# Late v, half masks, transposes in two PSUM banks, and two more chunks transposed by the crossbar, in a fused retention and Mish feed-forward kernel

## The chip, the core and the metric

One core of one Trainium2 chip. The time is the device time of one execution in microseconds (us). The kernel before takes 314.44 us (median of 3 runs, 314.15 to 315.28). A difference of under 2% counts as "same".

## The reference, cut to what matters

```python
# q, k, v: (8 batches, 8 heads, 576 positions, 64)
scores = q @ k.T / sqrt(64)
ret    = scores * Dmat[None]           # Dmat[h,i,j] = gamma_h ** (i-j) for i >= j, else 0
x      = (ret @ v) -> (4608 tokens, 512)
h = x @ w_in                            # 512 x 2048
g = h * tanh(softplus(h))               # Mish
out = g @ w_out                         # 2048 x 512, float32
```

The 576 positions are cut in chunks of 128 tokens, 36 chunks in all, two chunks of two batches being a pair (pair 7 is chunks 14 and 15). Inside a chunk the scores are computed whole; what earlier positions give comes through a running state (the sum of k times v). The feed-forward part runs over groups of four chunks, and it is nearly all of TensorE's work. A projection is full-width when it takes all 512 tokens of a group at once. In the first groups, where not all tokens are there yet, a chunk's own projections are cut in four quarters, between which other jobs are placed.

Of the kernel before, what the change touches and what calls it, by code (L numbers as in the profile page):

```python
# [11 lines left out]
BF16 = mybir.dt.bfloat16  # L12
# [5 lines left out]
def kernel(  # L18
# [30 lines left out]
    nF = d_ff // P  # L49
    KC = d_model // P  # L50
    NCH = 4
    NPE = 16


    chunks = []
# [69 lines left out]
    def load_w_in(f, nf):  # L125
        cols = ds(P * f, P * nf)
        nc.gpsimd.dma_start(out=w_in_t[:, :, cols], in_=w_in_r[:, :, cols])
# [19 lines left out]
    def await_load(n, x):  # L147

        m, u = divmod(n, 2)
        nc.gpsimd.tensor_copy(seen, pairs[m][x][0:1, u, H - 1, 0:1])  # L150

    def load_v(n):
        (b, i0, _), = chunks[n]
        nc.gpsimd.dma_start(out=pairs[n // 2]["v"][:, n % 2], in_=v[b, :, ds(i0, P), :].rearrange("h p d -> p h d"))
# [28 lines left out]
    mask1 = consts.tile([P, 2, NP, P], F32)  # L183
    for h in range(H):
        nc.scalar.activation(mask1[:, h // NP, h % NP, :], dif, AX.Exp, scale=log_g[h])
    load_v(0)

    pos = consts.tile([P, 5], F32)
    nc.gpsimd.iota(pos, pattern=[[P, 5]], base=0, channel_multiplier=1,
# [20 lines left out]
                            base=0, pattern=[[1, P]], channel_multiplier=-1)  # L210
    nc.gpsimd.tensor_copy(mask2, mask)
    nc.gpsimd.memset(mask2[0:64, 64:P], 0.0)
    load_v(1)

    st_sum = {}
    st_sb = {}
# [49 lines left out]
    def step_t(n):  # L266

        m, u = divmod(n, 2)
        r = pairs[m]
        if "qk" not in r:  # L270
            r["qk"] = tr.tile([P, 2, 2, NP, P], BF16, name="qkT", bufs=3)
        if n >= NPE:
            nc.sync.dma_start_transpose(out=r["qk"].rearrange("p i u n t -> p (i u n) t"),
                                          in_=r["qks"].rearrange("p i u h d -> p (i u h d)"))
            return
        tp = ps_sc.tile([P, 4, NP, P], BF16, name="sc")[:, 0:2]
        for i in range(2):
            flat = r["qks"][:, i, u].rearrange("p h d -> p (h d)")
            for p in range(NP):
                nc.tensor.transpose(tp[:, i, p, :], flat[:, ts(p, P)], ident)  # L280
        for i, copy in enumerate((nc.scalar.copy, nc.vector.tensor_copy)):
            copy(r["qk"][:, i, u], tp[:, i])  # L282

    def step_n(m):

        r = pairs[m]
        kp = ps_sc.tile([P, 4, NP, P], BF16, name="sc")[:, 0:2]
        for u in range(2):
            for p in range(NP):
                nc.tensor.transpose(kp[:, u, p, :], r["qk"][:, 1, u, p, :], ident)  # L290
        r["ks"] = tok.tile([P, 2, H, D], BF16, name="ks", bufs=2)
        for u in range(2):
            nc.vector.tensor_tensor(
                by_slots(r["ks"][:, u]), by_slots(kp[:, u].rearrange("p s (r d) -> p (s r) d", r=2)),
                gk[:, place(2 * m), :].rearrange("p (r s) -> p r s", r=2).unsqueeze(3).to_broadcast([P, 2, NP, D]),
                op=OP.mult)

    def step_s(n):

        m, u = divmod(n, 2)  # L300
        qk = pairs[m]["qk"]
        sc = scores_tile()
        for p in range(NP):
            for e in range(2):
                r = ds(64 * e, 64)
                nc.tensor.matmul(sc[:, e, p, :], lhsT=qk[r, 1, u, p, :], rhs=qk[r, 0, u, p, :],  # L306
                                 start=True, stop=True)
        sm = tr.tile([P, 2, NP, P], BF16, name="sm")
        nc.vector.tensor_tensor(  # L309
            sm.rearrange("p e n i -> p (e n) i"), sc.rearrange("p e n i -> p (e n) i"),  # L310
            mask1.rearrange("p e n i -> p (e n) i") if n < NCH else
            (mask if len(chunks[n]) == 1 else mask2).unsqueeze(1).to_broadcast([P, 2 * NP, P]), op=OP.mult)
        pairs[m][u] = (sc, sm)

    def step_k(m):

        if m >= n_pairs or len(chunks[2 * m]) > 1:
            return
        b, i0, _ = chunks[2 * m][0]
        ks, vs = pairs[m]["ks"], pairs[m]["vs"]  # L320

        if m < 6:
            st = ps_sc.tile([P, 2, 2, NP, 64], F32, name="sc")[:, 0]
        else:
            st = ps_h.tile([P, 2, NP, 64], F32, name="hp")
        for u in range(2):
            for p in range(NP):
                for e in range(2):
                    nc.tensor.matmul(st[ds(64 * e, 64), u, p, :], lhsT=ks[:, u, 2 * p + e, :],  # L329
                                     rhs=vs[:, u, 4 * e + p, :],  # L330
                                     start=(u == 0 and p == 0), stop=True, skip_group_check=True)
        if i0 == 0:
            st_sum[b] = tr.tile([P, 2, NP, 64], F32, name="st")
            nc.vector.tensor_copy(st_sum[b], st)
        else:
            nc.vector.tensor_tensor(st_sum[b], st_sum[b], st, op=OP.add)  # L336
        ssb = tr.tile([P, 2, NP, 64], BF16, name="ssb", bufs=6)
        (nc.vector.tensor_copy if m < 4 else nc.scalar.copy)(ssb, st_sum[b])  # L338
        for u in range(2):
            st_sb[b + u, i0 + P] = ssb[:, u]  # L340

# [37 lines left out]
        xt, s = x_of(n)  # L379
        nc.scalar.copy(xt[:, :, ts(s, P)].rearrange("p (e g) i -> p e g i", e=2), ot)  # L380

    def pair_o(m):

        sc = pairs[m][1][0]
        ot = sc.rearrange("p e (g u) i -> p e g u i", g=2)
        step_k(m)
        for u in range(2):
            within(pairs[m]["vs"][:, u], pairs[m][u][1], ot[:, :, :, u, :], u == 0)
        for u in range(2):
            across(2 * m + u, ot[:, :, :, u, :])  # L390
        xt, s = x_of(2 * m)
        nc.vector.tensor_copy(xt[:, :, ds(s * P, 2 * P)].rearrange("p n (u i) -> p n u i", u=2),  # L392
                              sc.rearrange("p e (g u) i -> p (e g) u i", g=2))


    gts = {}
# [70 lines left out]
    def one(n, steps):  # L467
        for step in steps:
            if step == "P":
                step_p(n // 2, (n % 2,))  # L470
            else:
                {"T": step_t, "S": step_s, "O": step_o}[step](n)

    def first(n, steps):
        for step in steps:
            if step in "qk":
                cast_first(n, "qk".index(step))
            elif step in "QK":
                turn_first(n, "QK".index(step))
            else:  # L480
                {"V": cast_v, "S": step_s, "O": step_o}[step](n)

    first(0, "qQkK")
    await_load(0, "k")
    load_v(2)
    first(1, "q")
    keep_warm(3)
    first(0, "VS")
    first(1, "Qk")
    keep_warm(3)  # L490
    await_load(1, "k")
    load_v(3)
    await_load(2, "q")
    load_w_in(0, 2)
    first(1, "K")
    first(0, "O")
    first(1, "V")
    first(2, "q")
    keep_warm(3)
    first(1, "S")  # L500
    first(2, "Qk")
    keep_warm(3)
    await_load(2, "k")
    load_w_in(2, 2)
    load_w_in(4, 4)
    load_w_in(8, 4)
# [26 lines left out]
    for i in range(4, nF):  # L533
        if i == 6:
            step_n(0)
        elif i == 8:
            step_k(0)
        elif i == 9:
            step_n(1)
        elif i == 10:  # L540
            one(4, "P")
        elif i == 12:
            one(4, "T")
        elif i == 13:
            one(4, "S")
        elif i == 14:
            one(5, "P")
        elif i == 15:
            one(4, "O")
        g1(0, i)  # L550

    load(6)
    for n in range(4, 8):
        for fb in range(4):
            if n < 7:
                if fb == 1:
                    one(n + 1, "T")
                elif fb == 2:
                    one(n + 1, "S")
                    if n % 2 == 0:  # L560
                        step_k(n // 2)
                    if n < 6:
                        one(n + 2, "P")
                elif fb == 3:
                    one(n + 1, "O")
            g1_chunk(n, fb)
    load(7)

    def visit(m, w):

        n = 2 * m
        if w == 0:
            if m > 4:
                step_p(m)
            if 2 * m + 2 < NPE:
                load(m + 4)
        elif w == 2:
            if m == 5:
                step_k(1)
            one(n, "T")  # L580
        elif w == 3:
            one(n + 1, "T")
        elif w == 5:
            one(n, "S")
            one(n + 1, "S")
        elif w == 7 and m < 6:
            pair_o(m)

    def cross(m):

        step_t(2 * m)
        nc.gpsimd.tensor_copy(seen, pairs[m]["qk"][0:1, 0, 0, 0, 0:1])  # L592
# [15 lines left out]
        g2(1, i)  # L608
    for i in range(nF):
        visit(6 + i // 8, i % 8)  # L610
        if i == 6:
            step_p(8)
        elif i == 8:
            cross(8)
            load(11)
        g1(2, i)
        if i % 8 == 7:
            pair_o(6 + i // 8)
            if i == 15:
                scores(8)  # L620
            for j in range(4):
                g2(1, 8 + i // 2 - 3 + j)
# [50 lines left out]
```

## The kernel before: what the change touches

Scores need q and k transposed. For the chunks from 4 up to `NPE` TensorE does it, from there on a crossbar transpose on SyncE's DMA queue:

```python
NPE = 16
def step_t(n):                                   # transposes of chunk n
    if n >= NPE:
        nc.sync.dma_start_transpose(out=r["qk"]..., in_=r["qks"]...)   # whole pair
        return
    tp = ps_sc.tile([P, 4, NP, P], BF16, name="sc")[:, 0:2]            # PSUM, one bank
    ...                                          # 2 x 4 TensorE transposes of 128x128
    for i, copy in enumerate((nc.scalar.copy, nc.vector.tensor_copy)):
        copy(r["qk"][:, i, u], tp[:, i])         # q's half by ScalarE, k's by VectorE
```

The start loads q and k on SyncE and v and the weights on GpSimd's queue, in an order that small waits on GpSimd (`await_load`) hold in place. In the third group of the feed-forward, small jobs are placed between projections (`w` counts them):

```python
def visit(m, w):
    if w == 0:
        if m > 4: step_p(m)                      # scale q and k of pair m (VectorE)
        if 2 * m + 2 < NPE: load(m + 4)          # loads of a later pair
    elif w == 2: one(2*m, "T")
    ...
def cross(m):                                    # crossbar transpose, GpSimd waits for it
    step_t(2 * m)
    nc.gpsimd.tensor_copy(seen, pairs[m]["qk"][...])

for i in range(nF):                              # third group: pairs 6 and 7
    visit(6 + i // 8, i % 8)
    if i == 6:   step_p(8)
    elif i == 8: cross(8); load(11)
    g1(2, i)                                     # first projection of 128 columns, Mish
    if i % 8 == 7:
        pair_o(6 + i // 8)                       # outputs of the pair
        ...
        g2(...)                                  # second projection; stores on SyncE
```

## Time and profile before

| | before |
|---|---|
| time, profiled run | 314.46 us (span 312.8) |
| TensorE busy | 300.0 us, 96% |
| VectorE, ScalarE busy | 123.4 and 136.0 us |
| granted TensorE clock | 1.00 |
| DMA share, 0 to about 95 us | near full |
| first scores / first projection / first full-width projection | 8.52 / 18.07 / 22.61 us |
| scores of chunks 14 / 16 / 18 start | 104.16 / 108.58 / 124.02 us |

A kernel that is 96% TensorE can gain only by closing TensorE's gaps or by taking work from it, and a part of a change that does not reach TensorE shows nothing. In the timelines (start, duration, engine and line, operation) PE is TensorE's matmuls, PEld its weight loads, DVE VectorE, ACT ScalarE, POOL GpSimd and SP SyncE; a q behind the name marks the engine's issuing queue, L273 is a line of the kernel, and brackets at the end give the idle time before an instruction and what ended it. First the chain that ended last, from the page: shares of the span by engine, then by line.

```profile
PE 89%; ACT 4%; DVE 3%; issue 2%; DMA 1%; SPq 1%; ACTq 0%; DVEq 0%
```

DMA is 1% of it. Second, the timeline of SyncE's queue where a pair is transposed: start, duration, engine and line, operation.

```profile
113.45 0.35 SPq L462 DMA_DIRECT2D out_dram<-res  x1
114.65 1.95 SPq L273 DMA_TRANSPOSE qkT<-qks  x1
```

### The profile page before, as it was taken

What the parts mean: (1) busy time and instruction counts of PE and PEld (TensorE: products, weight loads), DVE (VectorE), ACT (ScalarE), POOL (GpSimd) and SP (SyncE); (2) the same over time, 40 slices, a digit from 0 to 9 for tenths busy, and PEclk for the clock granted to TensorE, in tenths of its full rate; (3) what the DMA queues carried; (4) which work ended last, traced back from release to release, by engine and by line L of the source; (5) the groups of instructions that cost most, each with busy time, mean ns of one, the idle gap of its engine ahead of it and who ended that gap; (6) DMA issues with size and microseconds to landing.
All of it is one profiled execution on the core that took longest, in us unless ns stands there. A gap on an engine that the chain in (4) does not pass through costs nothing.

```text
span 312.8 us, 6059 instructions
## 1 busy us (share of the span) xinstructions
PE 300.0 (96%) x2601; PEld 157.2 (50%) x2637; DVE 123.4 (39%) x170; ACT 136.0 (43%) x237; POOL 78.6 (25%) x102
## 2 busy tenths in 40 slices
PE   6899989999999999999999999999999999999995
PEld 2355578655455545454545454545454544444444
DVE  3546465219768561626252526252525221000000
ACT  6665655422364633343434343434343433334311
POOL 6576573453340404040404040600000000000000
PEclk9999999999999999999999999999999999999999
DMA  6999999999998696959696959692313100000132
GB/s 180 255 186 226 198 207 226 201 232 248 214 230 103 132 174 141 168 137 169 142 165 143 160 144 159 138 160 63 90 47 88 48 34 36 34 34 36 40 81 80
DMA packets 71946, 43.38 MB, mean 139 GB/s; under 512 B 55664, under 2 KB 63088, under 8 KB 71920
## 3 DMA queue, kind: packets, MB, share of 16 engines
q0 software_dynamic: 43424, 26.22, 55.8%
q1 hardware_dynamic: 28352, 16.65, 20.6%
q8 instruction: 20, 0.33, 0.5%
q10 hardware_dynamic: 144, 0.13, 0.1%
q14 instruction: 6, 0.05, 0.0%
HBM read 36.70 MB, written 9.44 MB: 148 GB/s over the span
## 4 chain that ended last, share of the span: by engine, by line
PE 89%; ACT 4%; DVE 3%; issue 2%; DMA 1%; SPq 1%; ACTq 0%; DVEq 0%
PE hp L439 39%; PE hp L404 32%; PE hp L427 4%; PE sc L306 3%; PE sc L347 3%; ACT res L459 2%; PE sc L361 2%; DMA kraw<-in_k_dram 1%; PE sc L280 1%; PE hp L329 1%; PE hp L451 1%; DVE sm L309 1%; PE hp L415 1%; PE sc L329 1%; ACT qkT L282 1%
## 5 line engine op out<-in xcount | busy, mean ns | idle before, releaser
L439 PE MATMUL hp<-w_out_t,gT 128*128 128x512 bf16 x541 | 125.2, 379 | 1.2 <-issue 0.3
L404 PE MATMUL hp<-xT,w_in_t 128*128 128x512 bf16 x480 | 112.7, 379 | 1.3 <-DVE xT L392 0.4
L406 ACT ACTIVATE gT<-hp 128x512 bf16<-128x512 f32 x124 | 74.0, 597 | 36.6 <-PE hp L404 34.0
L439 PEld LDWEIGHTS <-gT 128*128 128x128 bf16 x560 | 53.3, 98 | 62.6
L404 PEld LDWEIGHTS <-w_in_t 128*128 128x128 bf16 x496 | 47.5, 97 | 57.1 <-DVE xT L392 0.9
L459 ACT COPY res<-hp 128x512 f32<-128x512 f32 x35 | 20.5, 585 | 98.4 <-PE hp L439 98.4
L309 DVE TENSOR_TENSOR sm<-sc,mask 128x1024 bf16<-128x1024 f32 x36 | 42.7, 1217 | 10.0 <-PE sc L306 10.0
L592 POOL COPY seen<-qkT 1x1 bf16<-1x1 bf16 x10 | 1.8, 176 | 121.9 <-DMA qkT<-qks 121.9
L336 DVE TENSOR_TENSOR st<-st,hp 128x512 f32<-128x512 f32 x8 | 5.5, 686 | 54.9 <-PE hp L329 54.9
L392 DVE CAST xT<-sc 128x1024 bf16<-128x1024 f32 x14 | 17.1, 1221 | 22.6 <-PE sc L361 22.2
L261 DVE TENSOR_TENSOR qks<-kraw,gk 128x512 bf16<-128x512 f32 x32 | 21.8, 683 | 1.7 <-DMA kraw<-in_k_dram 1.7
L261 DVE TENSOR_TENSOR qks<-qraw,gq 128x512 bf16<-128x512 f32 x32 | 21.8, 681 | 0.0
L112 POOL DMA_DIRECT2D qraw<-in_q_dram x16 | 17.2, 1075 | 13.9 <-DVE qks L261 9.1
L112 POOL DMA_DIRECT2D kraw<-in_k_dram x16 | 17.1, 1072 | 9.3 <-DVE ssb L338 3.7
L112 POOL DMA_DIRECT2D v<-in_v_dram x16 | 17.2, 1080 | 6.6 <-DMA kraw<-in_k_dram 2.5
L454 DVE COPY half<-hp 128x256 f32<-128x256 f32 x1 | 0.4, 425 | 43.8 <-PE hp L451 43.8
L427 PE MATMUL hp<-xT,w_in_t 128*128 128x128 bf16 x272 | 17.0, 219 | 0.0
L427 PEld LDWEIGHTS <-w_in_t 128*128 128x128 bf16 x272 | 15.5, 98 | 0.9 <-issue 0.2
L282 DVE COPY qkT<-sc 128x512 bf16<-128x512 bf16 x12 | 5.1, 422 | 23.4 <-ACT qkT L282 23.4
L429 ACT ACTIVATE gT<-hp 128x512 bf16<-128x512 f32 x17 | 10.1, 597 | 8.6 <-PE hp L427 8.6
L338 ACT CAST ssb<-st 128x512 bf16<-128x512 f32 x12 | 7.4, 618 | 14.3 <-DVE st L336 13.3
L306 PE MATMUL sc<-qkT 64*128 64x128 bf16 x288 | 11.9, 218 | 1.7 <-DVE qkT L282 1.5
(67 smaller groups left out, 163.6 us busy)
## 6 DMA issues: line engine op xcount, KB each, us to landing
out_dram<-res SPq DMA_DIRECT2D x31, 256.0 KB, 2.1
qraw<-in_q_dram POOLq DMA_DIRECT2D x12, 512.0 KB, 6.9
kraw<-in_k_dram POOLq DMA_DIRECT2D x12, 512.0 KB, 8.2
v<-in_v_dram POOLq DMA_DIRECT2D x12, 256.0 KB, 8.8
qraw<-in_q_dram POOLq DMA_DIRECT2D x8, 256.0 KB, 10.3
kraw<-in_k_dram POOLq DMA_DIRECT2D x8, 256.0 KB, 10.3
w_out_t<-in_moe_w_out_dram POOLq DMA_DIRECT2D x4, 512.0 KB, 11.7
qraw<-in_q_dram SPq DMA_DIRECT2D x8, 128.0 KB, 3.8
```

The source lines that it names most:

```text
L112: nc.gpsimd.dma_start(out=r[x][ds(off, ni)].rearrange("p u h d -> p (u h) d"), in_=src[ds(b, 2), :, ds(i0, ni), :].rearrange("b h p d -> p ...
L261: nc.vector.tensor_tensor(by_slots(r["qks"][:, i, u]), r[x][:, u].rearrange("p (r s) d -> p r s d", r=2), g[:, place(2 * m), :].rearrange( ...
L306: nc.tensor.matmul(sc[:, e, p, :], lhsT=qk[r, 1, u, p, :], rhs=qk[r, 0, u, p, :], start=True, stop=True)
L309: nc.vector.tensor_tensor(sm.rearrange("p e n i -> p (e n) i"), sc.rearrange("p e n i -> p (e n) i"), mask1.rearrange("p e n i -> p (e n) ...
L347: nc.tensor.matmul(ot[ds(64 * c, 64), e, g, :], lhsT=vs[:, h, :], rhs=sm[:, e, p, :], start=(start and g == 0), stop=True, skip_group_chec ...
L392: nc.vector.tensor_copy(xt[:, :, ds(s * P, 2 * P)].rearrange("p n (u i) -> p n u i", u=2), sc.rearrange("p e (g u) i -> p (e g) u i", g=2))
L404: nc.tensor.matmul(hp, lhsT=w_in_t[:, c, ts(f, P)], rhs=xts[t][:, c, :], start=(c == 0), stop=(c == KC - 1))
L406: nc.scalar.activation(gts[t][:, f, :], hp, AX.Mish)
L427: nc.tensor.matmul(hp[:, j, :], lhsT=w_in_t[:, c, ts(4 * fb + j, P)], rhs=xts[t][:, c, ts(s, P)], start=(c == 0), stop=(c == KC - 1))
L429: nc.scalar.activation(gts[t][:, ds(4 * fb, 4), ts(s, P)], hp, AX.Mish)
L439: nc.tensor.matmul(ops, lhsT=gts[t][:, f, ts(s, P)], rhs=w_out_t[:, f, :], start=(f == 0), stop=(f == nF - 1))
L459: copy(ot, ops)
```

## The change

Five intents. Load v of the first chunks behind their q and k, and multiply their masks in two halves, so that the next cast of k gets in between. Put q's and k's transposes in two PSUM banks, so that ScalarE and VectorE can copy at once. Give chunks 4 to 7 one more quarter between scores and outputs. Scale the next pair before the state sum (pairs 4 and 5). Take the transposes of 14 and 15 from TensorE. The core of the diff:

```diff
-    NPE = 16
+    NPE = 14
...
-    load_v(0)            # before the constants
+    await_load(0, "q")
+    load_v(0)            # v of 1, 2, 3 likewise one step later
...
-        tp = ps_sc.tile([P, 4, NP, P], BF16, name="sc")[:, 0:2]
+        tp = ps_sc.tile([P, 4, NP, P], BF16, name="sc")[:, ::2]
...
+        if between:      # chunks 0 and 1
+            for e in range(2):
+                nc.vector.tensor_tensor(sm[:, e], sc[:, e], mask1[:, e], op=OP.mult)
+                if e == 0:
+                    between()         # the next chunk's cast of k
...
-        (nc.vector.tensor_copy if m < 4 else nc.scalar.copy)(ssb, st_sum[b])
+        (nc.vector.tensor_copy if b < 4 and i0 < 2 * P else nc.scalar.copy)(ssb, st_sum[b])
...
-                if fb == 1:           # chunks 4 to 7: transposes, then scores,
+                if fb == 0:           # one quarter earlier
...
-            if m > 4:
-                step_p(m)
             if 2 * m + 2 < NPE:
                 load(m + 4)
...
-        elif w == 7 and m < 6:
-            pair_o(m)
+        elif w == 6 and m == 6:
+            step_p(7)
+        elif w == 7 and m < 6:
+            pair_o(m, lambda: step_p(m + 1))
...
-        if i == 6:
-            step_p(8)
-        elif i == 8:
+        if i == 8:
+            cross(7)
+            load(10)
+            step_p(8)
+        elif i == 10:
             cross(8)
             load(11)
```

More of the change, by code (lines that the diff above doesn't have):

```diff
@@ L212 @@
     nc.gpsimd.memset(mask2[0:64, 64:P], 0.0)
-    load_v(1)
+    await_load(0, "q")
+    load_v(0)
     st_sum = {}
@@ L296, in step_n, with step_s @@
                 op=OP.mult)
-    def step_s(n):
+    def step_s(n, between=None):
         m, u = divmod(n, 2)
@@ L308, in step_s @@
         sm = tr.tile([P, 2, NP, P], BF16, name="sm")
-        nc.vector.tensor_tensor(
-            sm.rearrange("p e n i -> p (e n) i"), sc.rearrange("p e n i -> p (e n) i"),
-            mask1.rearrange("p e n i -> p (e n) i") if n < NCH else
-            (mask if len(chunks[n]) == 1 else mask2).unsqueeze(1).to_broadcast([P, 2 * NP, P]), op=OP.mult)
+        if between:
[3 more added lines that the diff above has]
+                    between()
+        else:
+            nc.vector.tensor_tensor(
+                sm.rearrange("p e n i -> p (e n) i"), sc.rearrange("p e n i -> p (e n) i"),
+                mask1.rearrange("p e n i -> p (e n) i") if n < NCH else
+                (mask if len(chunks[n]) == 1 else mask2).unsqueeze(1).to_broadcast([P, 2 * NP, P]), op=OP.mult)
         pairs[m][u] = (sc, sm)
@@ L317, in step_k @@
         if m >= n_pairs or len(chunks[2 * m]) > 1:
-            return
+            return None
         b, i0, _ = chunks[2 * m][0]
@@ L331, in step_k, with step_sum @@
                                      start=(u == 0 and p == 0), stop=True, skip_group_check=True)
+        return b, i0, st
+    def step_sum(b, i0, st):
         if i0 == 0:
@@ L380, in step_o, with pair_o @@
         nc.scalar.copy(xt[:, :, ts(s, P)].rearrange("p (e g) i -> p e g i", e=2), ot)
-    def pair_o(m):
+    def pair_o(m, then=None):
         sc = pairs[m][1][0]
         ot = sc.rearrange("p e (g u) i -> p e g u i", g=2)
-        step_k(m)
+        state = step_k(m)
         for u in range(2):
@@ L391, in pair_o @@
         xt, s = x_of(2 * m)
-        nc.vector.tensor_copy(xt[:, :, ds(s * P, 2 * P)].rearrange("p n (u i) -> p n u i", u=2),
-                              sc.rearrange("p e (g u) i -> p (e g) u i", g=2))
+        xv = xt[:, :, ds(s * P, 2 * P)].rearrange("p (e g) (u i) -> p e g u i", e=2, u=2)
+        if m == 5:
+            nc.scalar.copy(xv[:, 0], ot[:, 0])
+            nc.vector.tensor_copy(xv[:, 1], ot[:, 1])
+        else:
+            nc.vector.tensor_copy(xv.rearrange("p e g u i -> p (e g) u i"), ot.rearrange("p e g u i -> p (e g) u i"))
+        if then:
+            then()
+        if state:
+            step_sum(*state)
     gts = {}
@@ L484 @@
     await_load(0, "k")
-    load_v(2)
+    load_v(1)
     first(1, "q")
     keep_warm(3)
-    first(0, "VS")
-    first(1, "Qk")
+    first(0, "V")
+    step_s(0, lambda: first(1, "k"))
+    first(1, "Q")
     keep_warm(3)
     await_load(1, "k")
-    load_v(3)
-    await_load(2, "q")
+    load_v(2)
     load_w_in(0, 2)
@@ L499 @@
     keep_warm(3)
-    first(1, "S")
-    first(2, "Qk")
+    step_s(1, lambda: first(2, "k"))
+    first(2, "Q")
     keep_warm(3)
     await_load(2, "k")
+    load_v(3)
     load_w_in(2, 2)
@@ L536 @@
         elif i == 8:
-            step_k(0)
+            step_sum(*step_k(0))
         elif i == 9:
+            one(4, "P")
             step_n(1)
-        elif i == 10:
-            one(4, "P")
         elif i == 12:
@@ L555 @@
             if n < 7:
-                if fb == 1:
+                if fb == 0:
                     one(n + 1, "T")
-                elif fb == 2:
+                elif fb == 1:
                     one(n + 1, "S")
-                    if n % 2 == 0:
-                        step_k(n // 2)
                     if n < 6:
                         one(n + 2, "P")
+                    if n % 2 == 0:
+                        step_sum(*step_k(n // 2))
                 elif fb == 3:
@@ L578, in visit @@
             if m == 5:
-                step_k(1)
-            one(n, "T")
-        elif w == 3:
+                step_sum(*step_k(1))
+            if n < NPE:
+                one(n, "T")
+        elif w == 3 and n < NPE:
             one(n + 1, "T")
```

## The prediction

> **What bounds the kernel now.** I read the page first (busy shares), then the waits of TensorE, then the timeline of the stages in which the change moves something. Two rows of the page, TensorE's busy time and the DMA engines' share in 40 slices:
>
> ```profile
> PE 300.0 (96%) x2601; PEld 157.2 (50%) x2637; DVE 123.4 (39%) x170; ACT 136.0 (43%) x237; POOL 78.6 (25%) x102
> ...
> DMA  6999999999998696959696959692313100000132
> ```
>
> TensorE is busy 300.0 of 312.8 us, so a change that removes no TensorE work can win 12.8 us at most. By stretch its idle time is 2.8 us in 0-10, 1.9 in 10-20, 2.0 in 20-60, 1.1 in 60-120, 1.4 in 120-300 and 3.5 after 300. The change touches nothing after 120 that TensorE waits for. The DMA row says something else: the transfer engines are full for the first 95 us or so. The waits of TensorE (line, releaser: us, times, longest):
>
> ```profile
> PE hp L244 <- DVE qks L234: 2.8, 3, 1.4
> PE sc L306 <- DVE qkT L282: 1.5, 4, 0.6
> ...
> PE sc L347 <- DVE sm L309: 0.3, 1, 0.3
> ```
>
> The first row is the start (k of the first chunks, cast behind loads and masks), the second the scores of chunks 4 to 7 behind the copies of the transposes. But the start ends at another gate. The timeline where the first full-width projection begins, and, from the DMA view, the weights it reads (512.0 KB, issued at 14.30):
>
> ```profile
> 21.68 0.88 PEld L427 LDWEIGHTS <-w_in_t 128*128 128x128 bf16 x15 [0.18 <-issue]
> ...
> 22.61 0.98 PEld L404 LDWEIGHTS <-w_in_t 128*128 128x128 bf16 x6
> ...
> w_in_t<-in_moe_w_in_dram POOLq DMA_DIRECT2D x1, 512.0 KB, 8.3
> ```
>
> 14.30 + 8.3 is 22.6: the weights land as their first load starts, and that load is not pulled ahead as the L427 ones are. TensorE arrives just in time for its weights, so an earlier arrival is worth nothing unless they come earlier too.
>
> **What the Trainium skill says.** (1) "DMA: Bandwidth & Descriptors", Issuing engines are not separate DMA queues: transfers from Sync and GpSimd run on the same 16 engines and interleave. The trace agrees: k of chunk 0 needs 4.0 us from issue to landing with v of chunk 0 in flight, q of chunk 0 needs 2.6. (2) "PSUM — Partial Sum Buffer", PSUM bank collisions raise a hardware error: ScalarE and VectorE may not read one bank at the same time, and software adds the wait. It agrees so far: each L282 copy on VectorE starts just after ScalarE's ends (31.59 + 0.58, then 32.20). (3) "TensorE: Matmul & The Clock Gate", Part 4, PE-mode transpose: the result lies in PSUM and must be copied out; about 275 ns each in one kernel's context. Here one takes 219 ns, and eight occupy 0.45 us of the chain. (4) "Perfetto Trace Analysis", Summary: the window of a hardware DMA leaves out the movement of the data. So a crossbar transpose is judged by its landing (4.5 us), not by its row of 1.98 us.
>
> **Part by part.**
>
> *v behind q and k, masks in two halves.* With v of chunk 0 gone from the first microseconds, I put k of chunk 0 at about 5.7 instead of 6.87 and the first scores at 7.3 instead of 8.52. The 1.22 us mask multiply between k's casts becomes one half of about 0.65 (two-operand instructions of 512 columns take 0.68), so the next k cast comes about 0.55 earlier. Not all of that arrives: the output matmuls of chunk 0 now wait for the second half, and the v cast stands in front of the next copies on ScalarE, with v landing at about 9 instead of 6.2. Walking the chain through, the first projection (L415) starts at about 17.2 instead of 18.07: 0.9 us gained. Then the gate. The bytes ahead of that weight load are the same 5.2 MB (2.1 of q and k, 1.05 of v, 2.1 of w_in in f32). The engines were near full from 3 us on, and leaving v out of 3 to 6 us wastes up to an estimated 0.5 to 0.9 us of transfer, partly regained in the gap around 17 us. So I expect these weights at 22.5, give or take 0.5, and TensorE waiting 0.5 to 1 us for them. Net of the start: 0, between -0.6 and +0.5.
>
> *Transposes in two banks.* In the built program VectorE's copy still waits for ScalarE's copy of the same transpose. 0.58 + 0.42 us stay in series, and the 1.5 us of waits of L306 stay. Moving the transpose one quarter earlier moves the scores as well, so the distance between them is the same. Gain 0.
>
> *Chunks 4 to 7.* Two quarters instead of one now lie between scores and output: the 0.32 us wait of L347 goes. But the state cast of the third pair moves from VectorE to ScalarE, between two activations. Before:
>
> ```profile
> 50.82 0.60 ACT L429 ACTIVATE gT<-hp 128x512 bf16<-128x512 f32 x1 [0.27 <-PE hp L427]
> 51.06 0.40 PE L306 MATMUL sc<-qkT 64*128 64x128 bf16 x8 [0.28 <-DVE qkT L282]
> ...
> 52.64 0.68 DVE L336 TENSOR_TENSOR st<-st,sc 128x512 f32<-128x512 f32 x1
> ...
> 53.35 0.43 DVE L338 CAST ssb<-st 128x512 bf16<-128x512 f32 x1
> ```
>
> The sum ends at 53.32. ScalarE, in order, would hold the cast (0.62) until 53.95 and the activation due at 52.87 until 54.55. With two projection banks, the fourth quarter of chunk 6, due at 54.12, waits about 0.5, and chunk 7, behind the copy of its x, another 0.3. Cost 0.8, net of this part +0.5.
>
> *Pairs 4 and 5.* The state sum goes behind the next pair's scaling (4 x 0.6 us on VectorE), and ScalarE's cast, which waits for it, holds two copies back: about 0.3 us for the second scores. In return x of pair 5 is copied half by ScalarE, half by VectorE; even in series, the first half releases the projection, and the 0.36 us for which L404 waits there goes. Sum 0.
>
> *Chunks 14 and 15 by crossbar.* 16 transposes leave TensorE: 2 x 0.45 = 0.9 us of the chain, with four copies that cost nothing. Before, SyncE and the scores of 14:
>
> ```profile
> 99.69 0.33 SPq L462 DMA_DIRECT2D out_dram<-res  x1
> 100.13 1.98 SPq L273 DMA_TRANSPOSE qkT<-qks  x1
> ...
> qkT<-qks SPq DMA_TRANSPOSE x1, 4.5
> ...
> 104.16 0.62 PE L306 MATMUL sc<-qkT 64*128 64x128 bf16 x16
> ```
>
> The new transpose stands behind that store in SyncE's order, and the store is only ready at 99.69. It would start at 100.1 and land at about 104.6. TensorE, with 0.9 less to do, is there at 98.84 + 5 x 0.87 = 103.2, and waits 1.4. The scores then start at 104.6 instead of 104.2: net +0.45. The transpose of pair 8 follows at 102.1, lands at about 106.6, and is needed at about 109: hidden.
>
> *After that* VectorE has x before the state sum. The sum's bank is free at about 141 in a period that needs it at 143.4, and the crossbar transposes land over 4 us early. Gain 0.
>
> Sum: 0 + 0.5 + 0 + 0.45 = about +0.9 us, or 315.4. Each of the three costs hangs on a few tenths of timing that I worked out by hand, and each is a place where the change was meant to win, so I lean back by half of it: 314.8.
>
> **Rivals.** *The start's gain gets through*: if the weights land by 21.7, because k of chunk 2 is earlier and so is every issue behind it, 0.9 us comes off, and the time is about 314. For it: the first weights of w_in are issued about 1 us earlier. Against: the second and third issues stand behind v of chunk 3, and the engines are full. *All waits go as intended*: the start wins 0.9, the L306 waits 1.2, L347 and x 0.7, the transposes 0.9: 3.7 us, 310.7. Against: the wait between the copies is still in the program, and the crossbar transpose cannot land by 103.2. *DMA becomes the bound*: v late starves ScalarE's queue, and the weights slip by 1 us or more: 316.5. For it: the full DMA row; against: the gap near 17 us.
>
> **Range and chances.** The start is worth -0.9 to +0.9, the other two net costs 0 to +0.5 each, and runs differ by up to 1 us (314.15 to 315.28). That gives 312.9 to 316.2 for eight cases in ten. Two per cent is 6.3 us: beyond the sum of every wait that the change aims at on the fast side, and more than any stall I can construct on the slow side. So 0.02, 0.96, 0.02.
>
> **What would show it.** Right: L415 starts near 17.2, yet the first full-width projection stays near 22.6 with a wait of 0.5 us or more before it; L306 still waits for VectorE's qkT copies four times; in chunk 6 and 7 TensorE waits for ScalarE where it had not; and the scores of chunk 14 wait over 1 us for the DMA transpose. Wrong: the full-width projection starts before 22.0 (the start does get through), no wait before the scores of 14 (the order on SyncE is not what holds it), or VectorE's copies starting with ScalarE's.

## The result, and the profile after

The changed kernel takes **316.26 us** (median of 4 runs, 316.04 to 316.77); the kernel before took 314.29 us beside it (4 runs, 314.13 to 315.28). The ratio is 1.0058, 95% interval 1.0034 to 1.0083: 0.6% slower, in the class "same". Ratios here and below are the mean time of one kernel's runs over that of the other's of the same rounds, so not quite the ratio of the medians. Executions over 1.5% slower than the fastest of the same kernel are left out of the means.

The page of the changed kernel: TensorE's busy time, the granted clock and the DMA share in 40 slices (7.9 us each), and the chain by engine.

```profile
PE 299.9 (95%) x2585; PEld 157.0 (50%) x2621; DVE 121.3 (38%) x170; ACT 134.8 (43%) x236; POOL 79.2 (25%) x103
...
PEclk9799999999999999999999999999999999999999
DMA  5999999999982999699797969793132300000032
...
PE 83%; DMA 6%; ACT 4%; issue 2%; DVE 2%; SPq 1%; ACTq 0%; DVEq 0%
```

TensorE has 16 instructions less, the transposes of 14 and 15, and the span still grew by 2.2 us. DMA now is 6% of the chain instead of 1%. The DMA row has a hole at slice 13 (about 94 to 102 us), and is a little fuller behind it, where before it went 6, 9, 6, 9. The waits of TensorE (line, releaser: us in total, times, longest) name the place:

```profile
PE sc L308 <- DMA qkT<-qks: 3.0, 2, 1.6
PE hp L246 <- DVE qks L236: 2.8, 3, 1.7
...
PE sc L308 <- DVE qkT L284: 1.2, 4, 0.3
...
PE hp L449 <- ACT gT L451: 0.2, 1, 0.2
```

The first row is new: scores that wait for crossbar transposes, twice. The timeline of TensorE shows which two:

```profile
104.83 0.62 PE L308 MATMUL sc<-qkT 64*128 64x128 bf16 x16 [1.43 <-DMA qkT<-qks]
...
126.38 0.62 PE L308 MATMUL sc<-qkT 64*128 64x128 bf16 x16 [1.61 <-DMA qkT<-qks]
```

These are the scores of chunks 14 and 18. The first wait was predicted, the second was not. SyncE's queue in the same stretch:

```profile
99.76 0.33 SPq L484 DMA_DIRECT2D out_dram<-res  x1
100.20 4.91 SPq L275 DMA_TRANSPOSE qkT<-qks  x2
114.12 0.34 SPq L484 DMA_DIRECT2D out_dram<-res  x1
115.93 6.01 SPq L275 DMA_TRANSPOSE qkT<-qks  x1
```

The transpose of pair 9, last line, starts 1.3 us later than before, takes 6.01 us of the queue instead of 1.95, and lands at 126.33 instead of 118.91. The stretch 110 to 120, first before, then after (its length, the busy time of PE, PEld, DVE, ACT and POOL, then granted clock, DMA share, which can pass 1, and GB/s):

```profile
110.00:120.00 10.00, 10.00 (x48) 4.53 (x47) 4.59 (x6) 3.21 (x6) 0.51 (x2) 1.00 0.95 147
```

```profile
110.00:120.00 10.00, 9.95 (x47) 4.52 (x47) 5.86 (x8) 3.59 (x6) 2.52 (x3) 1.00 1.36 204
```

The added traffic is the loads of pair 10. Before, they were issued at 87.9 to 91.3 and landed by 98.56. After, they are issued at 105.5, behind the wait for pair 7's transpose, and the loads of pair 11 follow at 109.1; the last of the six lands at 125.69, just before the transpose that had to move among the last four of them.

Where the 2.2 us of the two profiles came from, by the starts of the same instructions (the last column is what each step adds to the difference so far):

| milestone | before | after | added |
|---|---|---|---|
| first full-width projection | 22.61 | 23.42 | +0.81 |
| second projection of the first group | 57.84 | 58.26 | -0.39 |
| ninth projection of the third group | 98.84 | 98.91 | -0.35 |
| scores of chunk 14 | 104.16 | 104.83 | +0.60 |
| scores of chunk 18 | 124.02 | 126.38 | +1.69 |

**Theory A**: the crossbar part carries the loss (+0.6 and +1.7), in two mechanisms: the order on SyncE (chunk 14) and the moved loads (chunk 18). **Rival B**: the start carries it (+0.8 or more). The experiments separate them.

### The profile page after: what moved, and what is told of

Its sections match the earlier page's. It is cut to its first block, busy times and chain, and to the rows that moved or that the text cites. A ratio compares the mean times of both kernels' runs of the same rounds, so it can differ in the third digit from the quotient of the medians.

```text
span 315.0 us, 6021 instructions
## 1 busy us (share of the span) xinstructions
PE 299.9 (95%) x2585; PEld 157.0 (50%) x2621; DVE 121.3 (38%) x170; ACT 134.8 (43%) x236; POOL 79.2 (25%) x103
## 4 chain that ended last, share of the span: by engine, by line
PE 83%; DMA 6%; ACT 4%; issue 2%; DVE 2%; SPq 1%; ACTq 0%; DVEq 0%
PE hp L461 37%; PE hp L426 29%; DMA qkT<-qks 5%; PE hp L449 4%; PE sc L308 3%; PE sc L360 3%; ACT res L481 2%; PE sc L374 1%; SPq L142 1%; DMA kraw<-in_k_dram 1%; PE hp L338 1%; PE hp L473 1%; PE sc L282 1%; PE hp L437 1%; ACT qkT L284 1%
## 5 line engine op out<-in xcount | busy, mean ns | idle before, releaser
L411 DVE CAST xT<-sc 128x1024 bf16<-128x1024 f32 x13 | 15.9, 1224 | 97.3 <-PE sc L374 78.3
L318 DVE TENSOR_TENSOR sm<-sc,mask 128x1024 bf16<-128x1024 f32 x34 | 40.3, 1219 | 11.5 <-PE sc L308 11.5
L112 POOL DMA_DIRECT2D kraw<-in_k_dram x16 | 17.2, 1076 | 8.6 <-issue 4.1
L308 PEld LDWEIGHTS <-qkT 64*128 64x128 bf16 x288 | 8.2, 95 | 10.3 <-DMA qkT<-qks 3.6
L360 PE MATMUL sc<-sm,v 128*64 128x128 bf16 x288 | 12.2, 223 | 0.5 <-DVE sm L314 0.2
```

The lines of the kernel that those rows point to most:

```text
L112: nc.gpsimd.dma_start(out=r[x][ds(off, ni)].rearrange("p u h d -> p (u h) d"), in_=src[ds(b, 2), :, ds(i0, ni), :].rearrange("b h p d -> p ...
L308: nc.tensor.matmul(sc[:, e, p, :], lhsT=qk[r, 1, u, p, :], rhs=qk[r, 0, u, p, :], start=True, stop=True)
L318: nc.vector.tensor_tensor(sm.rearrange("p e n i -> p (e n) i"), sc.rearrange("p e n i -> p (e n) i"), mask1.rearrange("p e n i -> p (e n) ...
L360: nc.tensor.matmul(ot[ds(64 * c, 64), e, g, :], lhsT=vs[:, h, :], rhs=sm[:, e, p, :], start=(start and g == 0), stop=True, skip_group_chec ...
L411: nc.vector.tensor_copy(xv.rearrange("p e g u i -> p (e g) u i"), ot.rearrange("p e g u i -> p (e g) u i"))
```

## The experiments

Twelve kernels, all correct, all timed in five rounds. The first four ran beside one kernel before (314.63 us), the next four beside another (315.13), the next three beside a third (314.66), the last beside a fourth (314.61); the ratios take care of that. Times of different sessions differ by some tenths for the same kernel, so between sessions the ratios are compared.

### 1. The crossbar part alone, on the kernel before

```diff
-    NPE = 16
+    NPE = 14
 ... and visit, step_p(7), cross(7), load(10), step_p(8), cross(8) as in the change; nothing else
```

> The kernel before, with the crossbar part of the change alone: chunks 14 and 15 transposed by the crossbar, the loads of pair 10 issued after that transpose, pair 7 scaled two steps earlier, pair 8 one step later. Theory A (the crossbar part carries the loss: +0.5 by the wait for the transpose of pair 7, +1.6 by the wait for that of pair 9, which now runs amid the loads of pair 10): 2.0 to 2.3 us slower than before, scores of chunk 14 wait about 1.4 us and scores of chunk 18 about 1.6 us for a DMA transpose. Rival B (the start carries it): within 0.6 us of before, since the start is that of before. If the wait of chunk 18 does not appear, the collision needs the rest of the change too and theory A falls.

Measured: 317.89 us (316.64 to 319.91), ratio 1.0101 (1.0066 to 1.0136). The waits of the scores for crossbar transposes are 1.41 us (chunk 14) and 1.97 us (chunk 18). So the crossbar part alone loses as much as the whole change and more, and the start of the kernel before did not protect it. B falls as the main cause. The size is over the 2.0 to 2.3 expected, because the six runs split: three at 316.64 to 317.04 with a granted clock of 0.999 or 1.000 (+2.0 against the mean of the kernel before, +2.3 against its median), three at 318.75 to 319.91 with 0.992 to 0.995. The profile is one of the latter; per stretch its length, the busy time of PE, PEld, DVE, ACT and POOL, then granted clock, DMA share and GB/s:

```profile
127.00:130.00 3.00, 2.62 (x22) 1.31 (x24) 2.23 (x2) 0.00 (x0) 2.13 (x3) 0.76 0.07 14
130.00:133.00 3.00, 3.00 (x10) 1.12 (x9) 2.53 (x5) 0.00 (x0) 1.49 (x2) 0.67 0.94 214
```

The granted clock fell to 0.67 in the stretch from 130 to 133 us, behind the wait of 1.97 us, which ended at 127.33. The three runs with a low clock took 2.5 us longer than the other three. Whether the wait brought the fall is taken up at the end, and stays open.

### 2. The change without the crossbar part

```diff
-    NPE = 14
+    NPE = 16
 ... and visit, step_p(7), load(10), step_p(8), cross(8) as before
```

> The changed kernel with the crossbar part undone: TensorE transposes 14 and 15, loads and scaling placed as before. Theory A: 2.0 to 2.2 us faster than the changed kernel, so about 314.1 us, no wait for a DMA transpose before the scores of 14 and 18; what is left against before is the start (+0.8) less what the middle gives (-0.7), so within 0.4 us of before. Rival B: no more than 0.6 us faster than the changed kernel, still over 1 us slower than before.

Measured: 314.11 us (313.61 to 314.31), ratio 0.9972 (0.9953 to 0.9991), no wait for a crossbar transpose before chunks 14 and 18. The rest of the change is a gain of 0.9 us by the ratio (0.5 by the medians), near the 0.39 + 0.35 of the milestones and more than the 0.4 allowed. With experiment 1 this brackets the sum: +2.0 (undisturbed runs) or +3.2 (all) from the crossbar and -0.9 from the rest make +1.1 or +2.3, against +1.8 for the whole.

### 3. The loads of pair 10 issued early again

```diff
-            if 2 * m + 2 < NPE:
+            if 2 * m + 2 < 16:
                 load(m + 4)
...
             cross(7)
-            load(10)
```

> The changed kernel with one statement moved: the loads of pair 10 are issued at the head of the third block as before the change (about 88 to 91 us), not behind the transpose of pair 7. Theory A: the wait of the scores of 18 (1.61 us) goes, the transpose of pair 9 lands near 119 us again instead of 126, its row shrinks from 6.0 us to about 2, and the time falls by 1.4 to 1.7 us. The wait of chunk 14 (1.4 us) stays; it may grow by some tenths if the loads (landing at about 95 to 99) now delay the transpose of pair 7. Rival (the late transpose of pair 9 comes from something else, such as two transposes running in a row on SyncE): wait stays over 1 us, time within 0.5 us of the changed kernel.

Measured: 314.74 us (314.33 to 316.42), ratio 1.0000 (0.9976 to 1.0024), against 1.0058 for the changed kernel: 1.8 us won by moving three DMA issues (1.6 us if only runs with a clock of 0.999 or more are compared, of which the changed kernel has one). SyncE's queue and the scores of chunk 18 in its timeline:

```profile
100.10 4.75 SPq L275 DMA_TRANSPOSE qkT<-qks  x2
114.02 0.34 SPq L484 DMA_DIRECT2D out_dram<-res  x1
115.82 2.73 SPq L275 DMA_TRANSPOSE qkT<-qks  x1
```

```profile
124.59 0.62 PE L308 MATMUL sc<-qkT 64*128 64x128 bf16 x16
```

The transpose of pair 9 starts at the same time as in the changed kernel (115.82 against 115.93), behind the same two transposes in a row, but takes 2.73 us and lands at 120.22. The scores of chunk 18 start at 124.59 without a wait; the 1.43 us before chunk 14 stay. So the second wait is the collision with the moved loads, and the rival is out.

### 4. In addition, the transpose of pair 7 ahead of the store

```diff
+        if i == 7:
+            cross(7)
-        if i == 8:
-            cross(7)
+        elif i == 8:
             step_p(8)
```

> As the run before, and the crossbar transpose of pair 7 is emitted one step earlier, ahead of the output store in SyncE's order. Theory: it starts when pair 7 is scaled (about 96 us), lands at 100.5 to 102.5, before TensorE is there at 103.2, so the 1.4 us wait of the scores of 14 goes: 1.2 to 1.5 us faster than the run before, about 313.3 us. Rival (the transpose shares the engines with the loads of pair 10, which land until about 98.6, and takes 8 us or more from issue to landing, as the slow one of the changed kernel did): it lands after 103.2 and the gain is under 0.7 us.

Measured: 313.36 us (312.83 to 314.86), ratio 0.9962 (0.9936 to 0.9989). SyncE's queue and TensorE:

```profile
96.00 4.03 SPq L275 DMA_TRANSPOSE qkT<-qks  x1
100.14 0.53 SPq L484 DMA_DIRECT2D out_dram<-res  x1
100.77 2.35 SPq L275 DMA_TRANSPOSE qkT<-qks  x1
```

```profile
103.05 0.62 PE L308 MATMUL sc<-qkT 64*128 64x128 bf16 x16
```

The transpose starts at 96.00, shares the engines with the loads of pair 10 (4.03 us of queue), lands at 102.08, and the scores of chunk 14 come at 103.05 without a wait. The 1.4 us were the order on SyncE: the transpose had stood behind a store that was not ready until 99.7. With both repairs the crossbar part is no loss. Against experiment 2 (no crossbar), 0.9962 to 0.9972, it is worth 0.3 us with overlapping intervals, no more than its 0.9 us of TensorE work could give.

### 5. and 6. The start alone, and the order of the v loads alone, on the kernel before

```diff
 run 5                                        run 6: these lines only
-    load_v(0)                                -    load_v(0)
+    await_load(0, "q"); load_v(0)            +    await_load(0, "q"); load_v(0)
 ... v of 1, 2, 3 one step later              ... v of 1, 2, 3 one step later
-    first(0, "VS")
+    first(0, "V"); step_s(0, lambda: first(1, "k"))
 ... and chunk 1 likewise
```

> The kernel before, with the first part of the change alone: v of the first chunks loaded behind their q and k, masks of chunks 0 and 1 in two halves. The prediction (gain of 0.9 us at the first projection, swallowed by the weights' landing): first projection starts between 17.2 and 17.8 us, first full-width projection between 22.6 and 23.3 with a wait of 0.5 to 1 us for its weights; time within 0.6 us of before, rather slower (weights of the changed kernel and of the crossbar runs landed at 23.1 to 23.3, before at 22.6): +0.3. Rival B (the start costs 0.8 by itself): slower by 0.8 or more. Rival C (only the run with a granted clock below 1 in its first 20 us pays): runs with clock 1.000 equal to before, the others 0.4 us or more slower.

> The kernel before, with the order of the v loads alone, masks whole. If the later weights (landing near 23.2 instead of 22.6) are what the order of the loads costs, the time is that of the run with the whole first part, within 0.3 us, and the full-width projection starts at 23.0 to 23.3. If the half masks are what loses, this run is as fast as before or up to 0.3 us faster.

Measured: the start alone 315.00 us, ratio 0.9995 (0.9978 to 1.0012); the v order alone 314.89 us, ratio 0.9996 (0.9982 to 1.0010). Neither loses, neither gains. The start alone, from its timeline of TensorE:

```profile
17.76 0.81 PE L421 MATMUL hp<-xT,w_in_t 128*128 128x384 bf16 x4
...
22.93 0.39 PE L410 MATMUL hp<-xT,w_in_t 128*128 128x512 bf16 x1 [0.48 <-DMA w_in_t<-in_moe_w_in_dram]
```

The first projection starts at 17.76 (18.07 before, 18.28 with the order alone), and then the full-width one waits 0.48 us for its weights, which land at 22.89 in this run and at 22.87 with the order alone. This is the gate of the prediction. With the order alone TensorE came at 22.92 and did not wait. The weights' landing also differs from run to run with the same start: 22.56 in the kernel before, 23.15 in experiment 1, 23.33 in experiment 7, 23.66 and 22.17 in experiments 9 and 10. With late v it lay between 22.87 and 23.28 in the changed kernel and experiments 2 to 6. So the +0.81 of the milestones was one profile's picture, not a cost of the start, and rival B is out altogether. Of rival C there is one run to tell (315.68 us at a clock of 0.995, the highest of the six), which settles nothing.

### 7. The repaired kernel with the start of before

```diff
 experiment 4, with
-    await_load(0, "q"); load_v(0)
+    load_v(0)            # early, and v of 1, 2, 3 one step earlier; masks whole
```

> The run with the loads of pair 10 early and the transpose of pair 7 ahead of the store (313.36 us), with the start of the kernel before (v early, whole masks). If the start of the changed kernel costs what the landing of the weights says (22.6 against 23.1 us): 312.9 us, 0.3 to 0.6 faster than that run, the full-width projection starting at 22.6 without a wait. If the start is neutral: 313.2 to 313.5.

Measured: 313.06 us (312.76 to 313.76), ratio 0.9940 (0.9924 to 0.9955). That is between the two expectations; by the ratio it is 0.7 us better than experiment 4, with overlapping intervals. In its profile the weights landed at 23.33 and TensorE waited 0.27 us, so "22.6 without a wait" was a miss. One difference is visible: all six runs have a clock of 1.000, while two of six in experiment 4 had 0.994 and 0.995 and took 314.36 and 314.86 us. Without these two the mean of experiment 4 is 313.19 us, the same as here. So, as in experiment 5, no gain or loss of the start itself is seen.

### 8. v of chunk 3 behind the weights that gate the start

```diff
 experiment 4, with
-    load_v(3)
     load_w_in(2, 2)
     load_w_in(4, 4)
+    load_v(3)
...
-    first(3, "KV")
+    first(3, "K")
...
-    steps = {0: "S", 2: "O"}
+    steps = {0: "S", 1: "V", 2: "O"}      # the cast of v after the second projection
```

> The run with the loads of pair 10 early and the transpose of pair 7 ahead of the store (313.36 us), with v of chunk 3 loaded behind the weights that the first full-width projection reads, and its cast after the second projection in place of before the first. Theory (those weights are the gate of the start): 256 KB fewer lie ahead of them, at about 280 GB/s 0.9 us, so they land at 22.2 instead of 23.1, the wait of 0.7 us goes, and the time falls by 0.5 to 0.7 us, to about 312.8. Rival (the landing is set by how the queue's transfers share the engines, not by the bytes ahead, or v of chunk 3 now is late for its output): weights within 0.3 us of 23.1, or a wait for v near 20.5, and no gain.

Measured: 316.86 us (315.67 to 317.32), ratio 1.0048 (1.0027 to 1.0070). The weights landed at 21.58 instead of 23.08, below every other landing with late v (22.87 and later, as long as they went in one transfer), so their place in GpSimd's queue does set the gate. But v of chunk 3 slipped from 17.76 to 22.48, and the outputs of chunk 3 had to wait for it:

```profile
23.17 0.41 PE L360 MATMUL sc<-sm,v 128*64 128x128 bf16 x8 [2.87 <-ACT v L253]
```

The wait is not all of the loss: five of the six runs had a clock of 0.988 to 0.995, and in the profile the granted clock was 0.57 from 24 to 28 us, behind this wait. Half right and a clear loss: I had counted the bytes taken out from in front of the weights, and not those put in front of v.

### 9. and 10. The PSUM bank, and the PSUM tile

```diff
 run 9: experiment 7, with
-        tp = ps_sc.tile([P, 4, NP, P], BF16, name="sc")[:, ::2]
+        tp = ps_sc.tile([P, 4, NP, P], BF16, name="sc")[:, 0:2]
 run 10: experiment 7, with
+        tp = [ps_sc.tile([P, 4, NP, P], BF16, name="sc")[:, 0] for _ in range(2)]
```

> The best kernel so far (loads of pair 10 early, transpose of pair 7 ahead of the store, start of the kernel before; 313.06 us) with the transposes of q and k back in one PSUM bank. My reading: VectorE waits for ScalarE's copy because both copies read one PSUM tile, not because of the bank; so the bank does nothing: same within 0.3 us, the four waits of the scores for the k copies stay at 0.3 us each. Rival (the two banks help the copies run faster or the waits shorter): 0.5 to 1 us slower than 313.06, waits of 0.4 to 0.6 us.

> The best kernel so far (313.06 us) with q's and k's transposes of a chunk in two PSUM tiles in place of two banks of one tile. In the built program VectorE's copy then waits for the transposes alone. Theory: the two copies overlap, VectorE's starts 0.3 to 0.6 us earlier, and the four waits of 0.3 us before the scores of chunks 4 to 7 go: 0.8 to 1.2 us faster, 312.0. Rival (the second tile takes one of only three buffers of that pool, so transposes or scores wait for a buffer instead): new waits of TensorE before transposes or scores, gain under 0.3 us or a loss.

Measured: one bank 313.67 us (312.87 to 314.01), ratio 0.9960 (0.9941 to 0.9979); two tiles 313.13 us (312.54 to 314.11), ratio 0.9952 (0.9931 to 0.9972). With one bank the four waits of TensorE are 0.32, 0.28, 0.30 and 0.28 us, in experiment 7 with two banks 0.31, 0.28, 0.30 and 0.28: the bank does nothing for the waits. In time the one-bank run is 0.6 us slower than experiment 7, where I had said within 0.3, and that is in the rival's range; the intervals overlap a little. The profiles put their difference elsewhere: from the first full-width projection (23.38 with two banks, 23.70 with one) to the scores of chunk 14 (103.29 and 103.62) both take 79.9 us, and what differs lies before, where the one-bank run waited 0.72 us for its weights and experiment 7 0.27. With two tiles the four waits are gone. The copies of chunk 4, first two banks of one tile (experiment 7), then two tiles:

```profile
32.36 0.58 ACT L284 COPY qkT<-sc 128x512 bf16<-128x512 bf16 x1
...
32.97 0.42 DVE L284 COPY qkT<-sc 128x512 bf16<-128x512 bf16 x1 [1.55 <-ACT qkT L284]
```

```profile
31.36 0.42 DVE L284 COPY qkT<-sc 128x512 bf16<-128x512 bf16 x1 [0.90 <-PE sc L282]
31.40 0.58 ACT L284 COPY qkT<-sc 128x512 bf16<-128x512 bf16 x1
```

In the first, VectorE starts when ScalarE ends, released by ScalarE; in the second both start together, released by TensorE. The time barely moved, because the expected rival came true as well, at pair 5 in the two-tile run:

```profile
76.27 0.38 PE L282 MATMUL sc<-ident,qks 128*128 128x128 bf16 x4 [1.00 <-DVE st L349]
```

The second tile is one of only three buffers, and the transposes wait for a state sum to give it back. By the same two milestones: at the scores of chunk 7 the two-tile run is 1.45 us ahead of experiment 7, counted from the first full-width projection (25.40 against 26.85 us), at those of chunk 14 only 0.03 (79.88 against 79.91).

### 11. The gating weights in two transfers

```diff
 experiment 4, with
-    load_w_in(4, 4)
+    load_w_in(4, 2)
+    load_w_in(6, 2)
```

> The run with the late v, the early loads of pair 10 and the early transpose of pair 7 (313.36 us), with the weights that gate the start (four blocks of columns in one transfer) loaded in two transfers of two blocks. Prediction's gate: the first full-width projection needs the first of the four blocks only; two blocks are half the bytes (512 KB in f32 less, at about 290 GB/s 1.8 us), so the first half lands near 21.5, before TensorE is there at 22.4, and the wait of 0.5 to 0.9 us goes: 312.5 to 312.9 us. Rival (narrower transfers are slower, 1 KB runs in place of 2 KB, or later weights and v slip): a wait moves to the second half or to a later weight block, and the gain is under 0.3 us.

Measured: 313.23 us (312.59 to 313.25, 5 runs), ratio 0.9946 (0.9926 to 0.9966). The first half lands at 21.39, the second at 22.93, and no wait for weights is left. Against experiment 4 (0.9962) that is 0.5 us, within overlapping intervals, and the time missed the 312.5 to 312.9 expected. Without the two low-clock runs of experiment 4 nothing of it is left (313.19 on the mean, against 313.08 here), so a gain in time is not shown. This profile was one with a lower clock (0.995): the first projection started at 18.64 and the full-width one at 23.14, so here the weights were not the gate, TensorE was.

### 12. All of it together

```diff
 experiment 11, with
+        # two PSUM tiles for chunks 4 to 7, two banks of one tile for the later pairs
...
     first(1, "Q")
-    keep_warm(3)
+    keep_warm(7)         # filler matmuls, where TensorE waits for k of chunk 1
```

> The run with the late v, early loads of pair 10, early transpose of pair 7 and the weights in two transfers (313.23 us), with q's and k's transposes in two PSUM tiles for chunks 4 to 7 alone (not for the later pairs, where the second tile cost a wait of 1.0 us for a buffer), and with four more filler matmuls on TensorE before the transposes of k of chunk 1, where it idled 1.0 to 1.7 us. Theory: the four waits of 0.3 us go and stay gone (-1.2 to -1.4), and if the idle of TensorE is what lets its clock fall in the first 20 us, the granted clock is 0.998 or more in all runs (-0.1 to -0.8 in the runs that showed the fall): 311.5 to 312.2 us, below every run so far. Rival (the gain of two tiles is taken back at another buffer, and the filler delays the transposes of k of chunk 1): 312.8 to 313.5 us; the clock falls in some runs all the same.

Measured: **311.63 us** (311.11 to 312.58), ratio 0.9909 (0.9893 to 0.9926): 0.9% faster than the kernel before and 4.6 us below the changed kernel. That is within the expectation. All six runs have a clock of 1.000. From its timeline of TensorE, the first full-width projection and the scores of chunk 14:

```profile
22.39 0.81 PE L428 MATMUL hp<-xT,w_in_t 128*128 128x512 bf16 x3
```

```profile
101.37 0.62 PE L310 MATMUL sc<-qkT 64*128 64x128 bf16 x16 [0.47 <-DMA qkT<-qks]
```

TensorE is at the full-width projection at 22.39 and finds its weights there; in experiments 4 and 11 it was 23.13 and 23.14. The gain is over the other runs with late v: with the start of the kernel before, 22.43 was seen too (experiment 10). From there to the scores of chunk 14 it takes 78.98 us, against 79.91 in experiment 7, although chunk 14 now comes so early that it waits again, 0.47 us, for its transpose. What the filler, the split weights and the tiles give each was not timed apart.

## Why the prediction was right or wrong

It said 314.8 with a range to 316.2; measured were 316.26. The class was right, which was safe, as "same" reaches 6.3 us to either side; the value lies just outside the range. That it came so near is luck: the range was for the start and two small costs, and the loss came where the prediction had put nothing. Two slips in its sums do not matter: its own terms reach 316.3 on the slow side, not 316.2, and half of the 0.95 taken back gives 314.9.

- **The start: right.** "Net of the start: 0, between -0.6 and +0.5". Alone it measured 0.9995, and the gate was the one named: TensorE arrives earlier and waits for its weights, 0.48 us in experiment 5, 0.93 and 0.71 in experiments 3 and 4. The size of the earlier arrival was too hopeful: 17.76 where 17.2 was expected. The first scores did come at 7.12 in the changed kernel (7.3 expected, 8.52 before), but k of chunk 1 landed no earlier: at 9.59, against 9.47 before, its cast was done at 10.12, and a copy on ScalarE, behind v's cast, ended just after. So TensorE idled 1.68 us before the transposes of that k, and the clock granted from 10.2 to 13.8 us then was 0.57. Such a fall I had not considered. In this profile the first projection came at 18.75, and the full-width one at 23.42 without a wait: the weights, landed at 23.28, were not the gate there, and the sign of a wait of 0.5 us or more did not show.
- **Two banks: right**, gain 0. Experiment 9 shows that the bank does nothing for the waits, and experiment 10 that the wait hangs on the tile.
- **Chunks 4 to 7: wrong in sign**, +0.5 predicted, -0.39 measured. "The sum ends at 53.32" was taken from the kernel before, although the change moves that sum a quarter earlier: it ended at about 52.5, ScalarE's cast was done at 53.18 instead of 53.95, and the stall was 0.22 us instead of 0.8. Besides, the longest of the four waits for the copies (0.6 us, chunk 6) shrank to 0.30. So 0.32 + 0.30 - 0.22 = 0.40 us are won.
- **Pairs 4 and 5: a size off.** The gain of 0.36 came, the cost of 0.3 measured 0.08 (the block of scores of 10 and 11 took 0.70 us instead of 0.62).
- **Chunks 14 and 15: right.** A wait of 1.4 us predicted, 1.43 measured; landing at about 104.6 predicted, 104.79 measured; net +0.45 against +0.60. Experiment 4 shows the cause given, the place behind the store.
- **"After that ... the crossbar transposes land over 4 us early. Gain 0": this is the step that failed**, and with it "The change touches nothing after 120 that TensorE waits for". It is 1.69 us in the profiles, more than the whole distance of 314.8 from 316.26. The transpose of pair 9 landed at 126.33, and TensorE waited 1.61 us for it. The distance was read from the kernel before (118.91 against 124.02), as if the transfers around it stayed. They did not: a condition on `NPE` in an unchanged line moved the loads of pair 10 by 17.7 us (87.9 to 105.5) into the stretch of this transpose. Experiment 3 puts them back and takes 1.8 us off. The prediction's rivals named DMA as a bound only for the start.

The clock remains open. Runs with a mean clock of 0.988 to 0.995 came in most sets, unevenly: 16 of 39 with late v and half masks (the changed kernel and experiments 2, 3, 4, 5, 8 and 11; five of six in experiment 8), none of six with late v and whole masks (experiment 6), none of six with four more filler matmuls (experiment 12); with v early three of six in experiment 1, one of six in experiment 10, none in 7 and 9, and one of 44 of the kernel before.

In each of the five profiles with a fall it came behind an idle time of TensorE: 1.45 us (experiment 2), 1.66 (11), 1.68 (the changed kernel), 1.97 (1) and 2.87 (8). But in the changed kernel the 1.61 us before the scores of chunk 18 brought none (1.00 from 127 to 133 us), nor did the 1.43 us in the kernel before. And a clean set of six says little: without experiment 8, whose fall came elsewhere (after 24 us), the rate is 11 of 33, at which six runs would come out clean by luck in about one case in eleven, and experiment 6 was clean without the filler. So that idleness brings the fall is likely, not shown.

Nor is its price plain: the runs with a low clock took 2.5 us longer than the others in experiment 1, 1.8 in 3 and 1.4 in 4, but 0.4 in 2 and 0.1 in the changed kernel (three runs against one).

## What to carry to other kernels

When a constant changes, follow it through the lines that the diff does not show: here it moved three loads, and the loads cost more than the change could win. A crossbar transpose has to be judged in the traffic of its new neighbours (1.95 us of its queue in one place, 6.01 in another), and by what stands ahead of it in its queue; slack read from the old profile holds only if the transfers around it stay where they were. Where two engines shall read the results of one producer at once, look in the built program for what the second one waits for: two banks of one tile were still one wait.

## What the Trainium skill lacked or had wrong

- "DMA: Bandwidth & Descriptors", Rules for kernel authors, says of a transpose beside ordinary DMAs that it "needs nothing". That holds for correctness (all runs were correct). It lacks the cost: behind six loads, four of which were still landing, a crossbar transpose of a pair took 6.01 us of its queue and 10.4 us from issue to landing, against 1.95 and 4.3 us in the kernel before; with three loads around it 4.03 and 6.1 us.
- "TensorE: Matmul & The Clock Gate", Why this matters for your kernels, warns of idle gaps over about 3 us. The profiles here show the granted clock at 0.57 (mean of 3.6 us) and 0.67 (mean of 3 us) behind gaps of 1.68 and 1.97 us, and at 1.00 behind one of 1.61. Whether the gap alone does it is open.
- "PSUM — Partial Sum Buffer", PSUM bank collisions raise a hardware error, speaks of banks. It lacks that the wait which software adds can hang on the tile: with two banks of one tile VectorE still waited for ScalarE's copy (0.3 us of TensorE, four times), with two tiles both copies started within 0.04 us of each other.
